# A two-layer attention and feed-forward kernel: x ahead of the weights, and two tiles turned on TensorE instead of by DMA

## The chip, the cores and the metric

The kernel runs on one core of one Trainium2 chip. The metric is the time of one execution on the device in microseconds (us). Medians over several executions are quoted, with the lowest and highest beside them.

A profile belongs to a single execution. The engines are named as the profile names them: PE is TensorE's matmuls, PEld its weight loads, DVE is VectorE, ACT is ScalarE, POOL is GpSimd, SP is the engine that issues most DMA transfers. "Filler" is this document's word for a matmul of the identity with itself, which computes nothing that is used.

## The reference, cut to what matters

```python
# x: 2048 x 512, H = 32 heads of 16, window W = 256, F = 1792
def A(x, wqkv, wo):                       # attention in a window of 256 positions
    q, k, v = split(x @ wqkv)
    s = where(mask, q @ k.T * 16 ** -0.5, -1e9)
    return merge_heads(softmax(s) @ v) @ wo
def B(x, w_gate, w_up, w_down):           # feed-forward
    return (sigmoid(x @ w_gate) * (x @ w_up)) @ w_down

x = x + A(layernorm(x)); x = x + B(layernorm(x))
x = x + A(layernorm(x)); x = x + B(layernorm(x))     # the same weights again
```

The core works on 16 tiles of 128 rows. The kernel turns (transposes) every normed tile and every attention output before it multiplies it.

## The kernel before

The kernel is written by a planner. While the program is built, the planner simulates the engines with fixed durations and decides at each simulated moment what TensorE gets next. The result is a fixed order of instructions. Four parts matter here.

**The choice of the next piece of work, and the fillers.** If nothing is ready by the planner's reckoning in the first 85 us, it issues four fillers:

```python
        if u is None:
            if pv and go > 300:
                return self.do_values(pv, spare)
            if spare and 1500 <= pl.now < 85000:
                self.keep_warm(min(spare, key=lambda i: self.bank_turn[i]))
                return True
            return False
# ...
    def keep_warm(self, bank):
        for i in range(4):
            nc.tensor.matmul(self.banks[bank][:, 0:P], lhsT=self.ident[:], rhs=self.ident[:], start=True, stop=True)
        pl.count(4)
        pl.matmul("d", 4 * 56)
```

**The loads.** q, k and v weights first, on ACT's queue; x on SP's queue; the other weights from planned moments on:

```python
        for i, k in enumerate("kqv"):
            self.has_wq[k] = load(self.wq[:, :, h], wq_src[:, :, h], D * D * 2, prio=0, queue="ACT")
        for t in range(0, NBG, 2):
            self.has_x[t] = self.has_x[t + 1] = load_x(self.xsb[:, t:t + 2, :], slice(t, t + 2), 2, 0)
        # ... the rest of x, then wo after=15000, then after=18000:
        for i in range(7):
            a = load(self.wg[:, :, h], wg_src[:, :, h], D * n * 2, after=18000 + 2 * i * gap)
            b = load(self.wu[:, :, h], wu_src[:, :, h], D * n * 2, after=18000 + (2 * i + 1) * gap)
```

**The norms.** The first four normed tiles are turned on TensorE, all later ones by a transposing DMA:

```python
        if key == ("p", 0, 0):
            # nc.tensor.transpose(...) x4 into PSUM, then a copy
        else:
            d = pl.dma(1190, P * D * 2, lambda: nc.sync.dma_start_transpose(
                out=self.xnT[key][0][:, :, o:o + P], in_=box["xn"][0][:]), [c.done], prio)
```

**The attention outputs.** They come out of TensorE turned, with the softmax sums in extra columns. So there is one transposing DMA, a division on VectorE, and a second transposing DMA ahead of the output projection:

```python
        b = pl.dma(1800, 262144, turn, [box[0], box[1]], 3)            # OTs -> Oq
        c = pl.task({"DVE": 960}, norm, [b.done], 4, ...)              # Oq -> On
        d = pl.dma(1190, 131072, turn2, [c.done], 3)                   # On -> OnT
        # when d lands: self.oprojs.append(self.oproj_unit(L, t, box["OnT"]))
```

The softmax here doesn't subtract the row's maximum and nothing guards it: scores larger than these inputs give would overflow.

## Time and profile before

| Before | |
|---|---|
| time, median of 4 | 565.6 us (564.0 to 566.9) |
| span of the profiled execution | 560.8 us |
| TensorE busy | 545.8 us (97%) |
| fillers, all before 80 us | 320, 23.2 us busy |
| TensorE's waits of over 0.15 us, all with a named cause | 9.9 us |
| first gate/up matmul | 61.6 us |
| mean clock of TensorE | 0.999 |

The time of an execution is about 1.7 us more than its span. The profiled execution took 562.5 us, which is below every timed run of this kernel in its session, so a difference of two traces understates the gain by some 3 us. I read timed runs for how much, and traces for where.

The table is to be read as follows. TensorE is the bound, and 23 us of what counts as its busy time is waste. It lies at the start, where the work has a long chain of dependences: x, norm, q and k, scores, exponentials, values, output, second norm, gate and up. The views that show this are in the prediction.

Lines of the program have moved by the change. The filler is line 1039 before and 1104 after; transposes of normed tiles 524 and 529; gate/up 641 and 659; down 674 and 692; values 910 and 929; scores 831/841 and 850/860; output projection 701 and 720; exponentials 883 and 902.

### The profile page before, as it was taken

The numbers are of one execution on the slowest core, as the hardware profiler recorded it, in microseconds if no ns is written. First come the engines' busy times: TensorE is split into PE (matmuls) and PEld (weight loads), VectorE is DVE, ScalarE is ACT, GpSimd is POOL, SyncE is SP. The second block draws the span as 40 slices with busy tenths as digits, with TensorE's granted clock in tenths as the row PEclk, the third lists the DMA queues.
The fourth block names the chain that finished last, engine by engine and source line by source line (L and its number), as shares of the span: only waits on it lengthen the run. The fifth ranks groups of instructions, "written<-read, shape, count | busy, mean of one in ns | idle before, by whom it ended". The sixth has DMA issues, their size and how long they took to land.

```text
span 560.8 us, 24161 instructions
## 1 busy us (share of the span) xinstructions
PE 545.8 (97%) x10880; PEld 361.6 (64%) x10880; DVE 398.2 (71%) x864; ACT 410.3 (73%) x483; POOL 68.1 (12%) x157
## 2 busy tenths in 40 slices
PE   6999999899999999999999999999999999999997
PEld 5457766565766676566466765666557666767773
DVE  5779867887779878757986498866767566757432
ACT  1788878887978878868798877977778787853321
POOL 7202010121011021000210021000100000101000
PEclk9999999999999999999999999999999999999999
DMA  9588412354322223122521124222350314233000
GB/s 289 136 196 224 68 27 55 68 82 65 52 50 41 49 52 60 32 41 50 105 41 42 31 55 83 31 45 56 73 93 21 41 42 85 49 41 68 20 19 29
DMA packets 108679, 37.99 MB, mean 68 GB/s; under 512 B 85792, under 2 KB 108576, under 8 KB 108576
## 3 DMA queue, kind: packets, MB, share of 16 engines
q1 hardware_dynamic: 106992, 34.87, 31.5%
q8 instruction: 85, 1.39, 1.1%
q10 hardware_dynamic: 1584, 1.57, 0.9%
q14 instruction: 18, 0.15, 0.1%
HBM read 9.70 MB, written 2.10 MB: 21 GB/s over the span
## 4 chain that ended last, share of the span: by engine, by line
PE 83%; DVE 5%; DMA 4%; ACT 4%; issue 2%; POOL 1%; SPq 0%; ACTq 0%; DVEq 0%; POOLq 0%
PE bank L641 32%; PE bank L674 17%; PE bank L910 8%; PE Sps L831 6%; PE bank L701 5%; PE bank L562 5%; PE bank L616 4%; PE bank L584 4%; ACT PTring L883 3%; DMA xnT<-xn 2%; PE Sps L841 2%; DVE st L490 1%; DVE PTring L769 1%; DMA xsb<-in_A_x_dram 1%; DMA Oq<-OTs 1%
## 5 line engine op out<-in xcount | busy, mean ns | idle before, releaser
L883 ACT ACTIVATE PTring<-Sps 128x2048 bf16<-128x2048 f32 (+1 forms) x122 | 225.9, 1852 | 31.4 <-PE Sps L831 30.0
L641 PE MATMUL bank<-xnT,wg 128*128 128x256 bf16 (+1 forms) x952 | 139.4, 267 | 1.8 <-DMA xnT<-xn 1.7
L641 PE MATMUL bank<-xnT,wu 128*128 128x256 bf16 (+1 forms) x952 | 140.0, 267 | 0.0
L656 DVE SCALAR_TENSOR_TENSOR hT<-th,bank 128x256 bf16<-128x256 bf16 x224 | 86.7, 416 | 40.7 <-ACT th L653 40.2
L674 PE MATMUL bank<-wd,hT 128*128 128x512 bf16 x448 | 112.3, 380 | 0.3 <-ACT OTs L546 0.3
L653 ACT ACTIVATE th<-bank 128x256 bf16<-128x256 f32 x224 | 78.6, 389 | 39.7 <-PE bank L641 37.7
L641 PEld LDWEIGHTS <-wg 128*128 128x128 bf16 x952 | 85.9, 98 | 27.2 <-issue 5.0
L641 PEld LDWEIGHTS <-wu 128*128 128x128 bf16 x952 | 87.9, 98 | 14.0 <-issue 1.4
L495 POOL TENSOR_SCALAR st<-st 128x1 f32<-128x1 f32 x64 | 18.8, 294 | 449.2 <-DVE st L491 449.2
L769 DVE TENSOR_TENSOR PTring<-PTring,mask 128x1024 bf16<-128x1024 bf16 x64 | 44.0, 688 | 38.5 <-ACT PTring L883 38.4
L674 PEld LDWEIGHTS <-hT 128*128 128x128 bf16 x448 | 42.2, 98 | 41.2 <-issue 2.3
L883 ACT ACTIVATE edge<-Sps 128x2048 bf16<-128x2048 f32 (+1 forms) x32 | 56.8, 1775 | 12.7 <-PE Sps L841 12.5
L546 ACT CAST OTs<-bank 128x512 bf16<-128x512 f32 x49 | 36.0, 735 | 35.8 <-PE bank L910 32.7
L910 PEld LDWEIGHTS <-Vaug 128*32 128x32 bf16 x2880 | 44.4, 97 | 17.2 <-issue 15.5
L910 PE MATMUL bank<-PTring,Vaug 128*32 128x64 bf16 (+1 forms) x2880 | 52.9, 203 | 0.4
L831 PE MATMUL Sps<-qT,kTp 32*128 32x64 bf16 (+3 forms) x1856 | 48.1, 218 | 0.9 <-ACT PTring L883 0.8
L769 DVE TENSOR_TENSOR edge<-edge,maske 128x1024 bf16<-128x1024 bf16 x60 | 40.6, 684 | 8.5 <-ACT edge L883 8.4
L490 DVE BATCH_NORM_STATS2 st<-xsb 128x6 f32<-128x512 bf16 x64 | 43.8, 685 | 3.2 <-DMA xsb<-in_A_x_dram 2.9
L910 PE MATMUL bank<-edge,Vl 128*32 128x64 bf16 x1024 | 44.6, 193 | 0.0
L831 PEld LDWEIGHTS <-kTp 32*128 32x128 bf16 x1856 | 24.7, 92 | 27.3 <-issue 23.9
L496 POOL TENSOR_TENSOR st<-st,nhalf 128x1 f32<-128x1 f32 x64 | 41.0, 641 | 5.3
L910 PE MATMUL bank<-edge,Vh 128*32 128x64 bf16 x896 | 41.1, 193 | 0.0
(66 smaller groups left out, 561.7 us busy)
## 6 DMA issues: line engine op xcount, KB each, us to landing
Vl<-Vaug SPq DMA_DIRECT2D x32, 68.0 KB, 2.2
out_dram<-xsb SPq DMA_DIRECT2D x32, 64.0 KB, 1.9
Vh<-Vaug SPq DMA_DIRECT2D x28, 68.0 KB, 2.2
wg<-in_B_w_gate_dram SPq DMA_DIRECT2D x7, 256.0 KB, 4.3
wu<-in_B_w_up_dram SPq DMA_DIRECT2D x7, 256.0 KB, 4.2
wd<-in_B_w_down_dram SPq DMA_DIRECT2D x2, 896.0 KB, 6.3
wq<-in_A_wqkv_dram ACTq DMA_DIRECT2D x3, 512.0 KB, 4.7
xsb<-in_A_x_dram SPq DMA_DIRECT2D x6, 256.0 KB, 6.3
```

The lines of the kernel that those rows point to most:

```text
L490: nc.vector.bn_stats(out=st[:, 0:6], in_=self.xsb[:, t, :])
L496: nc.gpsimd.tensor_tensor(out=st[:, 8:9], in0=st[:, 9:10], in1=self.nhalf[:], op=ALU.pow)
L546: self.nc.scalar.copy(out=out, in_=in_)
L562: return [(mm_ns(TGW), lambda kt=kt: nc.tensor.matmul(self.banks[bank][:], lhsT=self.wq[:, kt, cq * P:cq * P + P], rhs=self.xnT[key][0][:, ...
L641: return [(mm_ns(w), lambda i=i, j=j, fc=fc, wt=wt, kt=kt: nc.tensor.matmul(pt[:, i, j, :], lhsT=wt[:, kt, fc * P:(fc + 1) * P], rhs=self. ...
L653: nc.scalar.activation(out=box["th"][0][:], in_=pt[:, 0, :], func=AF.Tanh, scale=0.5)
L656: nc.vector.scalar_tensor_tensor(out=self.hT[:, chunk, :], in0=box["th"][0][:], scalar=1.0, in1=pt[:, 1, :], op0=ALU.add, op1=ALU.mult)
L674: nc.tensor.matmul(self.banks[bank][:], lhsT=self.hT[:, c, o:o + P], rhs=self.wd[:, fc, :], start=fc == 0, stop=fc == FC - 1)
L769: done = pl.task({"DVE": dve_bf_ns(1024)}, lambda e: nc.vector.tensor_tensor(out=r, in0=r, in1=m.to_broadcast([P, 16, HP]), op=ALU.mult), ...
L831: nc.tensor.matmul(self.sps[:, m, o:o + n * HP], lhsT=kTp[32 * m:32 * m + 32, i, tt, e, :], rhs=self.qT[32 * m:32 * m + 32, i, q0:q0 + n * ...
L883: nc.scalar.activation(out=out, in_=src, func=AF.Exp, scale=scale)
L910: nc.tensor.matmul(o, lhsT=Va[:, c0:c0 + 32], rhs=p(h), start=k == 0 or t == 0, stop=k == len(parts) - 1 or t == 0, tile_position=(0, 32 * g))
```

## The change

Its intent: shorten the dependent chain at the start. x goes out ahead of q, k and v weights, on two queues; the bulk weights follow at once, gate and up weights in larger pieces and down weights in smaller ones; the first two tiles' outputs and second norms are turned on TensorE. Constants are set on VectorE before the work starts, and a few priorities and planned durations move. The diff, cut to its core:

```diff
-PACE = (2900, 3200)
+PACE = (2700, 3000)
-FETCH = (1200, 800)
+FETCH = (1200, 1300)
# loads
+        for t in range(0, NBG, 2):
+            self.has_x[t] = self.has_x[t + 1] = load_x(self.xsb[:, t:t + 2, :], slice(t, t + 2), 2, 0, ("SP", "ACT"))
         for i, k in enumerate("kqv"):
-            self.has_wq[k] = load(..., prio=0, queue="ACT")
-        for t in range(0, NBG, 2):
-            self.has_x[t] = self.has_x[t + 1] = load_x(self.xsb[:, t:t + 2, :], slice(t, t + 2), 2, 0)
+            self.has_wq[k] = load(..., prio=0, queue="ACT" if i < 3 else "SP")
-        self.has_wo = load(self.wot[:], wo_src, D * D * 2, after=15000)     # then 7 + 7 pieces from 18000
+        gap, at = 1300, 4000
+        self.has_wo = load(self.wot[:], wo_src, D * D * 2, after=at)        # then 2 + 2 halves right behind
# constants: the memsets of Vaug and half of those of Vd, formerly tasks of GpSimd
+        for V in self.Vaug:
+            nc.vector.memset(...16:VS], 1.0)
+            nc.vector.memset(V[:, :, VS * H:VW], 0.0)
-        self.pl.free["DVE"] = 1500.0
+        self.pl.free["DVE"] = 3200.0
# norms
-        if key == ("p", 0, 0):
+        if key == ("p", 0, 0) or key[0] == "g" and self.by_pe(key[1], t):
# first q and k unit: tile by tile (128 columns) instead of 512 columns
+        by_tile = L == g == 0 and cq < 1
# down weights: halving folded into the residual add
-                out=self.xsb[:, t, :], in0=self.xsb[:, t, :], in1=self.banks[u.bank][:], op=ALU.add), [u.done], 1)
+                out=self.xsb[:, t, :], in0=self.banks[u.bank][:], scalar=0.5, in1=self.xsb[:, t, :], ...
# attention outputs
+        if self.by_pe(L, t):
+            self.turn_by_pe(L, t, box)      # 8 transposes, divide from PSUM, 4 transposes, copy
+            return
+    def by_pe(self, L, t):
+        return L * NT + t < 2 or L * NT + t >= 2 * NT - 0
# pick: values also go ahead when the previous exponential has no planned end yet
+        held = s < len(self.visits) and s > 0 and self.exps[s - 1].ends is None
-        if pv and (wait <= 600 or wait > 1e8):
+        if pv and (wait <= 600 or wait > 1e8 or held):
# the first visit's pace: 3000 -> 2500; narrow gate/up pieces for the first four tiles instead of two
```

## The prediction

> **What bounds the kernel now.** I read, in this order: the page's engine shares and chain, the stretches of the trace for the filler matmuls alone, TensorE's waits, a piece of steady timeline, and the first attention output's way through the DMA queue. The page first:
>
> ```profile
> PE 545.8 (97%) x10880; PEld 361.6 (64%) x10880; DVE 398.2 (71%) x864; ACT 410.3 (73%) x483; POOL 68.1 (12%) x157
> ...
> PE 83%; DVE 5%; DMA 4%; ACT 4%; issue 2%; POOL 1%; SPq 0%; ACTq 0%; DVEq 0%; POOLq 0%
> ```
>
> TensorE is busy 545.8 of 560.8 us and carries 83% of the chain that ended last. No other engine passes 73%. So the end moves only if TensorE's own stream gets shorter. But is the busy time useful? The program has a helper (line 1039) that multiplies the identity by itself, four matmuls at a time, whenever its build-time planner finds nothing to issue in the first 85 us. The same stretches view, for that line alone (columns: stretch, its length, PE busy with its count, weight loads, clock, DMA share, GB/s):
>
> ```profile
> 0.00:10.00 10.00, 7.02 (x76) 6.84 (x76) 1.00 0.86 265
> 10.00:20.00 10.00, 0.39 (x4) 0.27 (x4) 1.00 0.56 176
> 20.00:30.00 10.00, 1.22 (x16) 1.06 (x16) 1.00 0.78 204
> 30.00:40.00 10.00, 3.03 (x48) 2.68 (x48) 1.00 0.74 200
> 40.00:60.00 20.00, 10.31 (x160) 9.04 (x160) 1.00 0.90 189
> 60.00:80.00 20.00, 1.22 (x16) 1.06 (x16) 1.00 0.23 43
> ```
>
> All 320 fillers lie before 80 us and take 23.2 us: that is what the slow start costs, beside what is really idle. The reader should see two holes: 76 fillers before x arrives, and 160 between 40 and 60 us, when the DMA engines are 0.90 busy with weights and the first tile's feed-forward has not begun. True idle time of TensorE is small:
>
> ```profile
> PE bank L524 <- DVE xn L512: 4.5, 4, 2.2
> PE bank L641 <- DMA xnT<-xn: 1.7, 2, 1.1
> PE bank L1039 <- POOL ident L428: 1.4, 1, 1.4
> PE Sps L841 <- ACT PTring L883: 1.2, 4, 0.5
> PE Sps L831 <- ACT PTring L883: 0.8, 1, 0.8
> PE bank L674 <- ACT OTs L546: 0.3, 1, 0.3
> ```
>
> That is 9.9 us, of which 4.5 wait for the first four normed tiles. After that TensorE runs at its rate:
>
> ```profile
> 260.55 0.60 PE L641 MATMUL bank<-xnT,wu 128*128 128x256 bf16 x4
> 260.99 0.60 PE L641 MATMUL bank<-xnT,wg 128*128 128x256 bf16 x4
> ...
> 265.02 0.59 PE L674 MATMUL bank<-wd,hT 128*128 128x512 bf16 x2
> 265.55 0.41 PE L841 MATMUL Sps<-qT,kTp 32*128 32x64 bf16 x32
> 265.89 1.90 PE L616 MATMUL bank<-wq,xnT 128*128 128x512 bf16 x8
> 267.63 0.59 PE L674 MATMUL bank<-wd,hT 128*128 128x512 bf16 x2
> ```
>
> Four 256-wide matmuls start every 0.44 us (109 ns each), eight 512-wide take 1.74 us (217 ns each), and a change to another kind of matmul costs about 0.1 us (0.53 us for two 512-wide before the score matmuls, against 0.43). There is nothing to win in the middle except by fewer matmuls.
>
> Why the second hole: the first tile's output waits on transposes in the DMA queue.
>
> ```profile
> 38.28 1.46 SPq L928 DMA_TRANSPOSE Oq<-OTs  x1
> ...
> 43.67 0.35 DVE L934 RECIPROCAL Rt<-Oq 128x32 f32<-128x32 bf16 x1
> 44.05 0.69 DVE L935 TENSOR_TENSOR On<-Oq,Rt 128x512 bf16<-128x512 bf16 x1
> 44.77 1.19 SPq L939 DMA_TRANSPOSE OnT<-On  x1
> ```
>
> 5.4 us pass from the first issue to its reader, 4.6 from the second (the o-projection starts at 49.34), and on the chain the normed tile then takes "57.34 4.18 DMA xnT<-xn" before gate/up starts at 61.56.
>
> **What the Trainium skill says.** (1) "TensorE: Matmul & The Clock Gate", Part 1 (the HAM clock gate): a cold array runs at half clock, 107 ns per 128-wide matmul, and after some 3.4 us of activity at 56. The trace agrees: the first 76 fillers cost 7.02/76 = 92 ns on average, the 72 between 40 and 50 us 4.5/72 = 62 ns in busy time (neighbours start 56 ns apart). (2) The same page, Part 4 (PE-mode transpose): about 390 ns alone, about 275 in a kernel, output to PSUM, so a copy follows. The trace has 219 ns for line 524's transposes, which sit 56 ns apart; I use the trace. (3) "DMA: Bandwidth & Descriptors", Issuing engines are not separate DMA queues: the same 16 engines serve both queues; a second issuer saves issue time only. So what helps x is going ahead of the weights rather than its second queue. The trace fits: the four 128 KB x loads took a median 5.0 us to land while 1.5 MB of weights were loading beside them. No page bears on the planner.
>
> **The change part by part.** The middle part is set by a planner, so I compared the instruction order of the two built kernels and counted on TensorE, pricing by the rates above.
>
> - Fillers, first hole: 76 become 48. At 92 ns: 28 x 0.092 = 2.6 us off the path.
> - Fillers, later: 244 become 152. At 56 to 62 ns: 92 x 0.057 = 5.2 us off. They sit elsewhere too: before, 164 came when 23.7 to 29.9 us of useful matmul time had been issued, just ahead of gate/up; now 116 come at 11.9 to 15.6 us of it, around the first values matmuls, and only 32 later. Gate/up begins after 25.4 us of useful work and 180 fillers instead of 29.9 and 308. From the sums, 25.4 + 48 x 0.092 + 132 x 0.057 + 8 to 11 us of waits and switches (before: 61.6 - 29.9 - 7.0 - 13.2 = 11.5), I put it at 45 to 49 us, against 61.6.
> - Added on TensorE: 24 output transposes (16 + 8) and 8 for norms, 32 x 56 ns = 1.8 us, all on the path. Columns of real matmuls are unchanged: 32 of q and k become 128 wide from 8 of 512, and 56 x 4 more gate/up pieces are 128 wide instead of half as many at 256; 128-wide ones run at 56 ns, so this adds about 2 x 2.5 ns per pair, 0.3 us over 112 pairs. Kind changes go from 371 to 378: 7 x 0.1 = 0.7 us.
> - x ahead: the vector engine waits 2.9 us for x, until 7.2; 0.5 MB at the 265 GB/s seen there is 2 us, so landing should be near 4 to 5 us. But twelve memsets move to the vector engine ahead of it, the mask set-up (eight instructions, 2.2 us from 2.34 on before) now stands between the second and third normed tile, and q weights come later, behind x. So fillers end near 6 us, the first normed tile comes near 8, and the 4.5 us of waits there may stay. I credit 1 us. First scores, at 19.4 before, should come at 12 to 14.
> - DMA: six transposes fewer (4 of outputs, 2 of norms) of 124, which matter only early. The weights come in fewer, larger pieces and right behind; their bytes are the same. Waits at 60 to 140 us (the 1.7 us for xnT, and kin) may shrink by about 2 us: the planner now reckons 0.5 us more for a transpose that meets an instruction fetch, and the two early tiles no longer need the queue.
> - The down weights' halving, 2 x 1.08 us on DVE, folds into the residual add; the pace of attention visits goes from 2.9/3.2 to 2.7/3.0 us. Both are beside TensorE's work: attention ends earlier and leaves a longer feed-forward tail, with the same matmuls. Worth 0.
>
> Sum: -2.6 - 5.2 + 1.8 + 0.3 + 0.7 = -5.0, with -1 and -2 for waits -8.0, so 566.1 - 8.0 = 558 us.
>
> **The rivals.** (a) The wait moves: TensorE, with fewer fillers, idles instead, on the normed tiles at 6 to 12 us, on q weights, or on a late weight half behind 0.9 MB loads. For: x, weights and transposes share engines that were 0.74 to 0.90 busy to 60 us, and larger pieces make a transpose queue behind more bytes. Against: the planner counts loads and still left out 120 fillers. It would give back 3 to 6 us: 561 to 564. (b) The faster pace binds ScalarE or VectorE: ScalarE is about 81% busy at 200 to 300 us and would go to some 87%. Then TensorE would wait for exponentials (now 2.0 us in all). For: only four matmul banks. Against: there is feed-forward work to fill. It would cost 2 to 5 us: 560 to 563. (c) More is gained than the fillers tell: the start's 4.5 us of waits and the later 3 us both go. That would be 551 to 554.
>
> **Range and chances.** The counted part, -5, is firm; the rest is -7 to +5. Centre 558, range 551 to 563.5. Faster by over 2% needs under 554.8, so nearly all of rival (c): 0.24. Within 2%: 0.74. Slower by over 2% would need 577: 0.02.
>
> **What would show it.** Fillers x200 with about 13 us busy, 48 before 10 us; first score matmuls near 13 us; gate/up's first matmul at 45 to 49 us; TensorE's waits at 5 to 8 us, with xn still the largest; rates of 109 and 217 ns unchanged; gains already complete by 140 us, and equal progress after. I am wrong if gate/up begins early and the end does not follow, if TensorE waits over 3 us on weights, or if waits on exponentials pass 4 us.

## The result, and the profile after

| | before | after |
|---|---|---|
| time, median of 4 | 565.6 us (564.0 to 566.9) | 556.4 us (555.6 to 557.3) |
| span of the profiled execution | 560.8 us | 555.0 us |
| fillers | 320, 23.2 us | 200, 15.7 us |
| TensorE's waits of over 0.15 us | 9.9 us | 7.2 us (1.9 of them without a named cause) |
| first score matmuls | 19.4 us | 14.6 us |
| first gate/up matmul | 61.6 us | 47.3 us |
| mean clock | 0.999 | 0.994 |

The ratio of the times is 0.9839, with a 95% interval of 0.9808 to 0.9871. A ratio is the mean time of one kernel's fast runs over the mean of the other's in the same rounds, so it is not quite the quotient of the two medians. The gain is about 9 us or 1.6%: real. The predicted 558.0 (551.0 to 563.5) holds it.

The page of the kernel after, its line of busy times, its clock in 40 slices of 13.9 us and the chain's shares by engine:

```profile
PE 543.1 (98%) x10928; PEld 361.3 (65%) x10928; DVE 406.4 (73%) x893; ACT 402.3 (72%) x468; POOL 65.3 (12%) x145
...
PEclk8999899999999999999999999999999999999999
...
PE 90%; DVE 5%; issue 1%; ACT 1%; POOL 1%; DMA 1%; SPq 0%; ACTq 0%; DVEq 0%
```

TensorE's share of the chain rose from 83% to 90%, and DMA's fell from 4% to 1%: four transposing DMAs between 57 and 122 us, 17.7 us in all, lay on the path of before that sets the end. The first of them belongs to one of the two tiles that are now turned on TensorE. The two 8s in the clock's row are new. The kernel before has 9 in all 40 slices.

The fillers alone (line 1104), in the stretches that the prediction shows of before:

```profile
0.00:10.00 10.00, 5.62 (x52) 5.30 (x52) 0.99 0.78 242
10.00:20.00 10.00, 0.00 (x0) 0.00 (x0) 0.83 1.14 323
20.00:30.00 10.00, 3.41 (x52) 2.99 (x52) 1.00 1.12 251
30.00:40.00 10.00, 4.26 (x64) 3.66 (x64) 1.00 0.90 243
40.00:60.00 20.00, 2.44 (x32) 1.96 (x32) 1.00 0.21 49
60.00:80.00 20.00, 0.00 (x0) 0.00 (x0) 0.91 0.12 23
```

The second hole, 160 fillers at 40 to 60 us, is down to 32; 52 more than before lie at 20 to 40 us instead. The last column (GB/s) shows that the weights now come by 40 us, at 243 to 323 GB/s, where the kernel before was still loading 189 GB/s at 40 to 60. But that isn't what closes the hole: in the trace of before the last gate/up weights had landed at 44.7 us, 17 us ahead of the first gate/up matmul, and below the hole closes with the old loads too.

The first output's way, in TensorE's timeline (start, duration, line, operation, operands, count):

```profile
36.11 0.61 PE L996 MATMUL bank<-ident,OTs 128*128 128x128 bf16 x8
...
38.06 0.40 PE L996 MATMUL bank<-ident,On 128*128 128x128 bf16 x4
...
39.38 0.81 PE L720 MATMUL bank<-wot,OnT 128*128 128x512 bf16 x3
```

From the first turn to the output projection it is 3.3 us, against 11.1 us before (38.28 to 49.34). The eight transposes take eight times 56 ns to issue, as the trace of before had it for those of the norms.

What TensorE waited for:

```profile
PE bank L529 <- DVE xn L517: 2.3, 2, 1.8
PE bank L929 <- issue: 1.9, 1, 1.9
PE bank L1104 <- POOL ident L438: 1.4, 1, 1.4
PE bank L659 <- ACT OTs L550: 0.5, 1, 0.5
PE bank L569 <- DMA xnT<-xn: 0.5, 1, 0.5
```

The waits on transposing DMAs ahead of gate/up are gone, and the one on normed tiles has halved. One is new, a pause of 1.9 us that ends at 63.4 us and waits for nothing that the profile shows ("issue"):

```profile
61.31 0.20 PE L929 MATMUL bank<-PTring,Vaug 128*32 128x64 bf16 x3
63.38 0.19 PE L929 MATMUL bank<-PTring,Vaug 128*32 128x64 bf16 x1 [1.86 <-issue]
```

It falls inside a group of four like matmuls: three have run, the fourth comes 1.9 us later. After it the clock is at half for 3.4 us (64.5 to 67.9); it is also at half at 9.9 to 13.3 us. A 16 KB transfer on an instruction-fetch queue starts at 60.7 and another at 64.4 us, which points to the supply of instructions.

A count over all fourteen traces says more. That queue made 85 transfers for the 21,760 matmuls and weight loads of the kernel before, so one carries 256. The waits view lists 19 TensorE waits for "issue" of over 0.15 us, in thirteen of the traces. In each of the 19, the number of TensorE instructions ahead of the pause is 193 to 195 more than a multiple of 256 (2,241 in five of them, at 59 to 70 us), and such a transfer had started 2.2 to 2.9 us before TensorE went on. So these pauses lie at the edge between two blocks of instructions. That the next block comes too late is the plain reading; no run moved an edge on purpose. Here the 256 instructions ahead of the pause had been used up in 1.8 us.

**Where the time went.** I added up the useful matmul time of each trace: the columns of every matmul but the fillers, at the 2.4 GHz of the Trainium skill, "TensorE: Matmul & The Clock Gate", Part 1 (the trace's 217 ns for 512 columns agree within 2%), a quarter of that for matmuls that run four abreast. The lead of the kernel after, at the same moment of both traces:

| at | 20 | 40 | 60 | 100 | 140 | 300 | 520 us |
|---|---|---|---|---|---|---|---|
| lead | +1.9 | -0.9 | +6.2 | +3.6 | +6.8 | +6.1 | +7.4 us |

1.7 us of the lead from 60 us on is the added transposes themselves. So 6 us are won by 60 us, 2.6 us are lost again between 60 and 100 (the 1.9 us stall and the half clock lie there), 3.2 us are won between 100 and 140, and from then on it stays between 4.7 and 7.6 us. The win at 100 to 140 us shows in the stretches of all engines (PE, PEld, DVE, ACT and POOL busy, clock, DMA share, GB/s), first the kernel before:

```profile
100.00:140.00 40.00, 37.02 (x859) 24.56 (x857) 32.16 (x75) 33.10 (x37) 7.35 (x16) 1.00 0.45 71
```

and after:

```profile
100.00:140.00 40.00, 40.00 (x1008) 24.84 (x1011) 36.54 (x82) 33.85 (x34) 8.88 (x18) 1.00 0.35 57
```

TensorE no longer pauses there at all. A sum of the terms fits the two spans: fillers -7.5, waits -2.7, added transposes +1.8, narrower matmuls and more changes of kind +1.0 (the prediction's figure, not a measured one), together -7.4. The two half-clock episodes, 6.8 us long, cost at most half of that, 3.4. So the sum lies between -7.4 and -4.0, and the spans differ by -5.8.

### The profile page after: what moved, and what is told of

It reads as the page before. It is cut to its first block, busy times and chain, and to the rows that moved or that the text cites. A ratio compares the mean times of both kernels' runs of the same rounds, so it can differ in the third digit from the quotient of the medians.

```text
span 555.0 us, 24233 instructions
## 1 busy us (share of the span) xinstructions
PE 543.1 (98%) x10928; PEld 361.3 (65%) x10928; DVE 406.4 (73%) x893; ACT 402.3 (72%) x468; POOL 65.3 (12%) x145
## 4 chain that ended last, share of the span: by engine, by line
PE 90%; DVE 5%; issue 1%; ACT 1%; POOL 1%; DMA 1%; SPq 0%; ACTq 0%; DVEq 0%
PE bank L659 34%; PE bank L692 18%; PE bank L929 8%; PE Sps L850 7%; PE bank L569 5%; PE bank L598 5%; PE bank L634 5%; PE bank L720 5%; PE Sps L860 2%; PE bank L1104 2%; DVE st L495 1%; DMA xnT<-xn 1%; DVE xn L517 1%; POOL st L501 1%; DVE PTring L788 0%
## 5 line engine op out<-in xcount | busy, mean ns | idle before, releaser
L671 ACT ACTIVATE th<-bank 128x256 bf16<-128x256 f32 x224 | 80.3, 388 | 62.1 <-PE bank L659 59.1
L692 PE MATMUL bank<-wd,hT 128*128 128x512 bf16 x448 | 114.3, 381 | 0.0
L659 PEld LDWEIGHTS <-wg 128*128 128x128 bf16 x1008 | 88.4, 98 | 28.5 <-issue 3.6
L659 PEld LDWEIGHTS <-wu 128*128 128x128 bf16 x1008 | 90.0, 98 | 13.7 <-issue 1.6
L500 POOL TENSOR_SCALAR st<-st 128x1 f32<-128x1 f32 x64 | 20.6, 321 | 422.9 <-DVE st L496 422.9
L550 ACT CAST OTs<-bank 128x512 bf16<-128x512 f32 x40 | 29.4, 736 | 24.4 <-PE bank L929 23.7
L929 PE MATMUL bank<-edge,Vl 128*32 128x64 bf16 x1024 | 44.7, 193 | 0.0
(71 smaller groups left out, 554.9 us busy)
```

The lines of the kernel that those rows point to most:

```text
L550: self.nc.scalar.copy(out=out, in_=in_)
L659: return [(mm_ns(w), lambda i=i, j=j, fc=fc, wt=wt, kt=kt: nc.tensor.matmul(pt[:, i, j, :], lhsT=wt[:, kt, fc * P:(fc + 1) * P], rhs=self. ...
L671: nc.scalar.activation(out=box["th"][0][:], in_=pt[:, 0, :], func=AF.Tanh, scale=0.5)
L692: nc.tensor.matmul(self.banks[bank][:], lhsT=self.hT[:, c, o:o + P], rhs=self.wd[:, fc, :], start=fc == 0, stop=fc == FC - 1)
L929: nc.tensor.matmul(o, lhsT=Va[:, c0:c0 + 32], rhs=p(h), start=k == 0 or t == 0, stop=k == len(parts) - 1 or t == 0, tile_position=(0, 32 * g))
```

## The experiments

Twelve kernels were run, each timed in five rounds beside the kernel before on the same chip; all gave correct results. The median of before was 565.7 us in each of the three sessions. One caution holds for all: any edit makes the planner lay out the whole program anew, and I allow a microsecond or two for that alone; no run measured it.

The theory was that the gain is the shorter start: fewer fillers and less waiting, carried unchanged to the end, with the TensorE turns as its largest part and x ahead as a smaller one. The rivals were that the pace of attention makes the gain or gives it back; that fillers themselves cost the time; and that much more is to be had at the start.

### Undoing one part

**Turns by DMA again.**

```diff
-        return L * NT + t < 2 or L * NT + t >= 2 * NT - 0
+        return False
```

> The changed kernel with only the TensorE turns of the first two tiles undone: their outputs and norms go through the DMA queue again. The built order holds 288 fillers against 200, the 88 extra ones just before gate/up, and 32 transposes fewer. Theory (the turns by TensorE close the second hole): +88 x 0.057 = 5.0 us, -1.8 us for the missing transposes, so about +3 us over the changed kernel, 559 to 560 us, and gate/up first at 51 to 54 us against 47.4. Rival (the loads and the pace gave the gain, the turns nothing): within 1 us of the changed kernel, 556 to 557.

Measured: 561.3 us (560.6 to 562.9), ratio 0.9929 (0.9908 to 0.9950). Fillers rose to 288 (21.5 us busy), the first output projection came at 49.1 us instead of 39.4, the first gate/up at 58.5 instead of 47.3. Within the full change the turns are worth about 5 us, where 3 were expected, and they are what brings gate/up forward: the new loads are all in this kernel, and the hole is open again.

**The old order of loads** (the load section of before in the kernel after).

```diff
-        # x first on SP and ACT, wq behind it, wo from 4000, halves of wg and wu right behind
+        # wq first on ACT, x on SP, wo from 15000, sevenths of wg and wu from 18000
```

> The changed kernel with the loads of before: weights of q, k, v at the same time as x, gate/up weights in sevenths with 1.6 us gaps from 18 us on, down weights in two halves last. The built order holds 188 fillers, 72 of them at the start. Theory (x ahead of the weights is worth the 24 fillers at the start, 2 to 2.5 us, and the early bulk weights little once the planner knows): +1 to +3 us, 557.5 to 559.5, first scores near 18 us instead of 14.6. Rival (order of the loads is most of the gain): +6 us or more. Rival (nothing): 556 to 557.

Measured: 558.7 us (556.8 to 559.5), ratio 0.9871 (0.9849 to 0.9892). First scores came at 19.1 us, nearly as late as in the kernel before, and still most of the gain is there. The first gate/up came at 49.0 us, and the fillers at 40 to 60 us are 48, against 160 before:

```profile
40.00:60.00 20.00, 3.50 (x48) 2.97 (x48) 1.00 0.52 152
```

So the turns close the second hole without the new loads. Within the full change the loads are worth about 2.5 us; that is weak, since the interval overlaps that of the kernel after (though not that of its repeat below).

**The old pace.**

```diff
-PACE = (2700, 3000)
+PACE = (2900, 3200)
-            return 2500
+            return 3000
```

> The changed kernel at the old pace of attention visits (2.9 and 3.2 us). Fillers 220 against 200. Theory (pace is beside TensorE's work): +20 x 0.057 = 1.1 us and no more, 556.5 to 558 us. Rival (the faster pace carries the gain): +4 us or more, 560 us and over. Rival (the faster pace costs waits on exponentials): faster than the changed kernel.

Measured: 556.5 us (555.7 to 557.5), ratio 0.9839 (0.9818 to 0.9860), equal to the kernel after. The pace is worth nothing that these runs can tell. In the trace of the kernel after, ScalarE's busy time at 200 to 300 us is 81.2 us, and it was 81.4 before.

**All early loads on one queue**, x still first.

```diff
-            ... load_x(self.xsb[:, t:t + 2, :], slice(t, t + 2), 2, 0, ("SP", "ACT"))
+            ... load_x(self.xsb[:, t:t + 2, :], slice(t, t + 2), 2, 0)
-            ... prio=0, queue="ACT" if i < 3 else "SP")
+            ... prio=0, queue="SP")
```

> The changed kernel with x and then the q, k, v weights all issued from one queue, in that order. Theory (what helps is that x goes ahead, the second issuer saves only issue time): first scores within 1 us of 14.6 to 15.6, total within 1 us of the changed kernel. Rival (the second queue brings bandwidth): first scores later by 2 us or more, total +2 us or more.

Measured: 556.9 us (554.7 to 558.2), ratio 0.9835 (0.9808 to 0.9863), first scores at 14.5 us. What helps x is going ahead; its second queue adds nothing that could be measured.

### One part alone, in the kernel before

**x ahead of the weights, on both queues, and nothing else.**

```diff
+        for t in range(0, NBG, 2):
+            ... load_x(self.xsb[:, t:t + 2, :], slice(t, t + 2), 2, 0, ("SP", "ACT"))
         for i, k in enumerate("kqv"):
             ...
-        for t in range(0, NBG, 2):
-            ... load_x(self.xsb[:, t:t + 2, :], slice(t, t + 2), 2, 0)
```

> The kernel before with one part of the change alone: the first four tiles of x go ahead of the q, k, v weights, on both queues. Fillers 304 against 320. Theory (x ahead alone brings the first scores forward, but the second hole swallows what is gained, because it ends when the first tile's output has gone through the DMA queue, behind the late weights): first scores at 14 to 16 us instead of 19.4, total only -0.5 to -2.5 us. Rival (an earlier start of 4 to 5 us carries to the end): total -4 us or more.

Measured: 563.7 us (561.4 to 565.0), ratio 0.9955 (0.9932 to 0.9977), so 2 us. First scores came 5.2 us earlier, at 14.2 us; but the first gate/up came at 64.9 us, later than the 61.6 of before. The second hole took the gain, and more than waiting was at work there. The last gate/up weights landed at 44.0 us (44.7 before), and the second transposing DMA of the first tile's output was issued at 43.65 us (44.77 before). But it took 7.5 us to land instead of 3.1, while 1.8 MB of down weights, issued at 39.8 us, were loading. Around its landing at 51.2 us TensorE did this:

```profile
51.51 1.92 PE L1039 MATMUL bank<-ident 128*128 128x128 bf16 x21 [2.38 <-issue]
...
53.91 2.47 PE L1039 MATMUL bank<-ident 128*128 128x128 bf16 x28
56.22 1.03 PE L701 MATMUL bank<-wot,OnT 128*128 128x512 bf16 x4
```

A pause of the kind described above ended, and then 49 fillers, in part at half clock (52.1 to 55.5 us), stood ahead of an output projection whose input had landed 5 us earlier. The place of a filler is fixed in the program, so when the real times differ from the planned ones it can hold up work that is ready.

**The turns on TensorE for two tiles, and nothing else** (the two new methods and the two branches, pasted into the kernel before).

> The kernel before with one part of the change alone: the outputs and norms of the first two tiles turned on TensorE. Fillers 224 against 320, 32 transposes more. Theory (this part is the larger one): 96 x 0.057 = 5.5 us less, 1.8 us more, so -3.5 to -5.5 us: 560 to 562 us, gate/up first at 49 to 54 us instead of 61.6. Rival (it needs the early weights too, and TensorE waits for the gate/up weights instead): under -2 us, with waits on wg or wu.

Measured: 577.3 us (575.0 to 578.3), ratio 1.0195 (1.0167 to 1.0223). It is 11.5 us *slower*, where a gain had been expected; the interval excludes 1, but reaches over the line of 2%, so the verdict is "unclear". The start did what it should: 224 fillers, first gate/up at 51.7 us, and at 100 us it leads the kernel before by 2.8 us of useful matmul time. At 120 us it is 3.3 us behind, at 140 it is 5.3 behind, at 300 it is 7.7 and at 420 it is 10.2. The stretch of the same 40 us as above:

```profile
100.00:140.00 40.00, 32.34 (x719) 21.89 (x711) 28.95 (x64) 28.60 (x30) 7.41 (x14) 0.83 0.38 65
```

TensorE is busy 32.3 us there instead of 37.0, and its clock is 0.83 on average. The waits of TensorE between 95 and 135 us, and its timeline:

```profile
PE Sps L830 <- ACT PTring L882: 4.9, 3, 2.3
PE bank L909 <- DVE PTring L768: 1.3, 1, 1.3
PE bank L640 <- DMA xnT<-xn: 1.1, 1, 1.1
```

```profile
102.42 0.41 PE L830 MATMUL Sps<-qT,kTp 32*128 32x64 bf16 x16 [2.31 <-ACT PTring L882]
104.86 0.61 PE L830 MATMUL Sps<-qT,kTp 32*128 32x64 bf16 x16 [2.04 <-ACT PTring L882]
```

Scores follow scores with nothing between them, each waiting for the exponentials of the one before to free its buffer. There is no feed-forward work to put there: it had been brought forward and was used up. ScalarE isn't short of time either, at 28.6 us busy of 40: it waits for the scores in its turn. Two half-clock episodes (103.3 to 113.5 and 130.6 to 134.0 us) follow the gaps. So starvation of TensorE is shown. Why the next piece of feed-forward came late is not: the chain of waits there has transposing DMAs of 3.9 to 4.6 us, for which this kernel's planner reckons less (its addition for an instruction fetch is still 800 ns, not 1300), and attention has its old start, so either may be behind it. A further 2.1 us is a pause at an instruction block's edge, at 521.7 us; the trace doesn't show whether it comes in every execution.

The parts do not add. x ahead alone gives 2 us and the turns alone cost 11.5; within the full change undoing the turns costs 5 us, the loads 2.5 and the pace 0.

### Are fillers a cost or a mark?

**Fillers only before 10 us of planned time**, in the kernel after.

```diff
-            if spare and 1500 <= pl.now < 85000:
+            if spare and 1500 <= pl.now < 10000:
```

> The changed kernel without any filler after 10 us of the plan (52 fillers instead of 200). Theory (fillers stand where TensorE would wait anyway; they mark lost time and are not its cause): the waits of TensorE grow by about the 8.5 us that the 148 fillers took, and the total does not fall; it may rise by 0 to 4 us where the idle time lets the clock fall to half. Rival (fillers push real work back): the total falls by 3 us or more.

Measured: 555.1 us (553.5 to 557.0), ratio 0.9816 (0.9792 to 0.9841), with 52 fillers instead of 200. The kernel after, run again unchanged in the same session, took 555.8. The 148 fillers that are gone left idle time in their places:

```profile
20.00:40.00 20.00, 16.36 (x257) 7.88 (x256) 14.08 (x25) 15.18 (x13) 1.13 (x2) 0.83 1.07 254
```

TensorE is busy 16.4 of these 20 us, with the clock at half from 29.9 to 36.8 us, and the end hardly moves.

**The same in the kernel before** (limit 13000 instead of 85000).

> The kernel before without any filler after 13 us of the plan (80 instead of 320). Theory: as above, the time stays lost: within +0 to +6 us of the kernel before, with half clock in the stretch from 40 to 60 us. Rival (240 fillers of 0.057 us cost 13.7 us by themselves): the total falls by 5 us or more.

Measured: 567.1 us (565.2 to 569.3), ratio 1.0024 (1.0003 to 1.0044), with 80 fillers instead of 320 and 22 us of waits instead of 10. Neither kernel gains by leaving them out. A filler mostly marks a moment with nothing to do (the run with x ahead alone shows an exception); the count of fillers measures the hole, and taking them away doesn't close it.

### What is left at the start

**The kernel after, again.**

> The changed kernel once more, unchanged. Is the stall of TensorE of 1.9 us at 61.4 us, in the middle of a values matmul group with nothing to wait for, and the half clock after it, part of the program or chance? If part: it comes again within 1 us of the same place. If chance (instruction supply): it is gone or elsewhere, and the span of this profile is some 3 us shorter or the same with another stall.

Measured: 555.8 us (554.9 to 556.4), ratio 0.9820 (0.9803 to 0.9838). The stall within a values group is there again (1.4 us at 62.2), this time without a half clock behind it. The early half clock lasted 6.8 us (7.9 to 14.7), first scores came at 15.6, and the wait for normed tiles was 3.2 us. So these three vary between executions of one program.

**The planner told when VectorE is really free.** The trace of the kernel after has VectorE's first statistics at 4.84 us, where the planner assumes 3.2.

```diff
-        self.pl.free["DVE"] = 3200.0
+        self.pl.free["DVE"] = 4800.0
```

> The changed kernel with the planner told that the vector engine is free at 4.8 us, as its trace shows, and not at 3.2: 16 more fillers stand ahead of the first transposes (64), so TensorE does not sit idle for 1.8 us at 6.7 us. Theory (that idle time lets the clock fall to half from 9.9 to 13.3 us, which costs about 1.5 us on the first k and q): the clock stays at full speed from 10 to 20 us, first scores at 13 to 13.8 us instead of 14.6, total -0.5 to -1.5 us. Rival (the vector engine's norms set the start, not the clock): clock mended, first scores still at 14.3 to 14.8, total within 0.4 us.

Measured: 564.0 us (561.5 to 565.8), ratio 0.9965 (0.9938 to 0.9991), nearly 8 us slower than the kernel after, though its first scores came earlier (13.7 us). Its timeline, all engines:

```profile
22.91 8.09 SPq L1127 DMA_DIRECT2D Vl<-Vaug  x2
...
29.77 0.59 ACT L550 CAST Vaug<-bank 128x512 bf16<-128x512 f32 x1 [6.95 <-DMA Vl<-Vaug]
...
32.19 0.56 PE L850 MATMUL Sps<-qT,kTp 32*128 32x128 bf16 x20 [6.37 <-ACT PTring L902]
```

Read it from the top. At 22.9 us a 68 KB copy out of the values buffer Vaug is issued, and it lands 6.8 us later; the median of these copies is 2.4 us in this run, but this one was issued amid the bulk loads. ScalarE's next eviction (the move of a result out of TensorE's bank) writes *another* tile's part of the same buffer, and waits for the copy for 6.95 us. ScalarE's next exponential stands behind that eviction, and the scores need the exponential: TensorE stops for 6.4 us. In the kernel after the same evictions stand ahead of the copy, so no one waits. The shift of the start changed only who comes first.

**The same, with the values buffer cut in two**, so that the copy and the next eviction touch different tiles.

```diff
-        self.Vaug = [big.tile([P, NBG, VW], BF16, name=...) for i in range(3)]
+        self.Vaug = [[big.tile([P, 2, VW], BF16, name=...) for j in range(2)] for i in range(3)]
```

> The run with the planner's vector engine at 4.8 us came out 8 us slower than the changed kernel, with TensorE idle 6.4 us at 25.6 us: ScalarE's eviction of one v tile waited 6.9 us for the copy of other rows of the same Vaug buffer, which took 6.8 us to land behind the bulk weights. This kernel is that one with each Vaug buffer cut into two buffers of two tiles, so eviction and copy share no buffer; TensorE's order is the same. Theory (that wait alone cost the 8 us): the 6.4 us stall and the half clock after it are gone, total back to 555 to 557.5 us. Rival (the earlier fillers or the new plan as such cost it): stays at 560 us or more.

Measured: 555.4 us (554.5 to 555.7), ratio 0.9811 (0.9785 to 0.9837). TensorE's waits:

```profile
PE bank L929 <- issue: 1.9, 1, 1.9
PE bank L1104 <- POOL ident L438: 1.4, 1, 1.4
PE bank L529 <- DVE xn L517: 0.9, 1, 0.9
```

The 6.4 us are gone, which shows the shared buffer as their cause. The wait for normed tiles is 0.9 us instead of 2.3, first scores at 13.6 us, gate/up at 45.2, and there was no half clock in this execution; the pause of 1.9 us at the block's edge is still there, at 59.2 us. Its ratio is the lowest of all, but its interval overlaps that of the kernel after (0.9803 to 0.9838 in the repeat). I don't call it better.

**A candidate**: the buffer cut in two, its constants set behind the first four norms, and VectorE's start at 3.6 us.

> Towards a better version: the changed kernel with Vaug cut in two as well, its six memsets and the mask set-up moved behind the first four norms on the vector engine, and the planner's start set to 3.6 us. Theory: the first bn_stats start near 4.0 us instead of 4.84 and the fourth normed tile comes 2 us sooner; first scores at 12.3 to 13.5 us instead of 14.6, TensorE's wait on xn under 1.2 us, no half clock before 14 us; total 553 to 555.5 us. Rival (what is saved at the start is lost again in the second hole, which ends with the first tile's output): within 0.7 us of the changed kernel.

Measured: 556.3 us (554.6 to 561.0), ratio 0.9836 (0.9799 to 0.9874). No gain: first scores came at 14.3 us, and the clock was at half from 10.2 to 13.6 us, both against what was expected. The statistics began at 3.90 us, a microsecond earlier; but the third then waited for the second half of x until 6.70 us. The landing of x sets the start there, not VectorE, so the rival "much more is to be had at the start" fails for this way of getting it.

## Why the prediction was right

The time and the mechanism were right: fewer fillers, ahead of an unchanged rate. That the total came so close is in part luck, as errors of the terms offset each other. Its steps in their order:

- **The bound.** TensorE stayed the bound, and the rates stayed: 56, 109 and 217 ns for 128, 256 and 512 columns.
- **Fillers, first hole.** The count of 48 was right (four more followed later within the first 10 us). The price was too low: 52 took 5.62 us, 108 ns each: the cold rate, which the clock column does not show so early. The 92 ns of before was a mean over a cold part and a warm one (its last fillers, from about 7 us on, are the fast ones), and it was the cold part that stayed. So the saving was 7.02 - 5.62 = 1.4 us, not 2.6.
- **Fillers, later.** 16.2 us became 10.1: a saving of 6.1 us, not 5.2, as those of before had cost more than the 57 ns assumed (16.2/244 = 66). Both together: -7.5 against -7.8 predicted. "About 13 us busy" was 15.7; the prediction's own saving, 23.2 - 7.8, would have made it 15.4.
- **Gate/up** at 45 to 49 us: 47.3, and 48.3 in the repeat.
- **Added work.** The 32 transposes are there. The 0.3 and 0.7 us were not measured: 2 x 2.5 ns on 112 pairs is 0.56 us, not 0.3, and counted by the shape of the array the two traces change kind 380 and 381 times, where the prediction had 371 and 378. The sum of terms closes with them, but within 3.4 us only.
- **x ahead.** First scores at 14.6 us (15.6 in the repeat), later than the 12 to 14 given: the early half clock was not foreseen. The credit of 1 us was small: the wait for normed tiles alone fell from 4.5 to 2.3 us.
- **DMA waits** between 60 and 140 us were credited with 2 us; the trace shows 3.2 us won at 100 to 140 us, and 2.6 lost at 60 to 100.
- **Pace, worth 0**: shown by the run with the old pace.
- **Gains complete by 140 us**: so it is, to some 2 us in the traces (a lead of 6.8 us at 140, 4.7 to 7.6 later).
- **The DMA engines and the weights.** They were 0.74 to 0.90 busy to 60 us but for 10 to 20 us, where its own lines have 0.56. The down weights come in smaller pieces, not larger.

Of the rivals, (a) came in small: 1.9 us of new pause, at the edge of an instruction block and not on the things that it named. (b) is refuted by the run with the old pace. (c) was not reached: 7.2 us of waits remain.

What the prediction missed is the middle of the story. It does not say what each part is worth alone, and the parts do not add. Counting fillers gave the turns alone a gain of 3.5 to 5.5 us (the expectation above), and they cost 11.5 us. The prediction was right for the change as a whole because it was counted from the order of the changed kernel, where the later starvation does not occur, and not from a sum of ideas. Open remain: the cause of the late feed-forward work in the run with the turns alone, why the block of instructions comes late near 61 us, and the share of the smaller edits (values ahead when held, narrow first pieces, the fetch constant, the folded halving, priorities), which no run undid singly.

## What to carry to other kernels

In a program whose order is fixed at build time, count waste such as fillers in the trace, but don't expect to win by deleting it: it mostly marks a hole in the dependences, and in these runs only shortening the chain closed it. Test parts of a change both ways, undone in the new kernel and alone in the old one; here one part was worth 5 us in one and cost 11.5 us in the other. When a start is moved, look for buffers that are shared by a slow copy and an unrelated writer: splitting one took away a 6.4 us stall. When TensorE pauses and no one is named, count its instructions to the pause: a fixed remainder by the block size points to their supply.

## What the Trainium skill lacked or had wrong

- "TensorE: Matmul & The Clock Gate", Part 1: it gives an idle window of about 3.4 us ahead of the half clock. Here the clock fell for 3.4 us after a stall of 1.9 us (kernel after, 61.3 us), and did not fall after stalls of 1.9 us (59.2 us, split buffer with the true start) and 1.4 us (62.2 us, the repeat). At the start, waits for normed tiles of 0.9, 1.8 and 3.2 us at the longest (split buffer, kernel after, its repeat) were followed by 0, 3.4 and 6.8 us at half clock, but waits of 2.2 us (kernel before) and 2.7 us (x ahead alone) by none. So shorter gaps can be enough, and not always. Every stretch at half clock amid the work lasted 3.4 us or two or three times that. That an activity window runs free, as the page says, would fit; no run shows it.
- The same page, Part 4: 275 to 390 ns for a 128 x 128 transpose, and a clock gate that does not open for them. The records here have 219 ns, and eight in a row start 56 ns apart, at the full rate, amid other matmuls. No run had transposes alone.
- "DMA: Bandwidth & Descriptors", Queues, rings and completion order: that each engine takes descriptors in ring order agrees with a 68 KB copy landing after 6.8 us behind the bulk loads, against a median of 2.4 us. What no page has is the consequence for a program: an eviction to another part of the copied buffer waited 6.95 us, and splitting the buffer removed it.
- "Runtime: NRT & Kernel Launch", Instruction fetch mechanics: it calls the refill of instructions mostly hidden. TensorE paused 1.4 to 2.1 us with no named cause within a values group between 59 and 70 us in six executions of the changed kernel and its variants, and 2.4 us at 49.1 us with x ahead alone. All 19 such waits in the traces, from 0.16 us up, lie 193 to 195 instructions past a multiple of 256 and end 2.2 to 2.9 us after the start of a 16 KB transfer on TensorE's instruction queue. That a block that comes late is behind them is the plain reading, and no run tested it.
